# The sixth group's output tails: turned ahead of the quadrant copies, spread by VectorE

## The chip, the cores and the metric

One core of one Trainium2 chip runs the whole kernel. The metric is the device time of one execution in microseconds; the time of a kernel is the median of its runs.

## The reference

```python
B, F, D, L = 16384, 26, 16, 6          # Din = min(F * D, 1024) = 416
def reference(x0, ws, bs):             # x0 (16384, 416), ws (6, 416, 416), bs (6, 416), all bfloat16
    x = x0
    for l in range(L):
        proj = jnp.einsum('bd,de->be', x, ws[l]) + bs[l]
        x = x0 * proj + x
    return x
```

Six layers of a cross network: each multiplies the current rows by a square matrix, adds a bias, multiplies elementwise by the input rows and adds the current rows.

## The kernel before

**Groups, jobs, tiles, tails.** The 16384 rows are eight groups of 2048. Group g in layer l is job (g, l); both count from 0, so the sixth group is g = 5, and its last layer is job (5, 5). On chip the activations are kept transposed: features on partitions, rows along the free dimension. 416 features are three blocks of 128 (tiles 0, 1 and 2 of a job) and a remainder of 32 features, the tail. 2048 rows are four chunks of 512, which is one PSUM bank. The tail of a group is one tensor of 128 partitions x 512: each of the four chunks has its 32 features in one quadrant of 32 partitions. In some groups the chunks change quadrants from layer to layer, and the old tail, which is the residual of the next layer, has to be copied to the new quadrants: `prefill` calls `rotate` (lines 445 and 446), two DMAs for a job on SyncE's queue. These are the quadrant copies.

**One chunk of a tile.** TensorE does 13 matmuls of 32 rows each (lines 1073 and 1077) into a PSUM bank; ScalarE adds the bias and writes a work buffer `tw` (line 551; there are four such buffers, one for a tile); for each pair of chunks VectorE multiplies by x0 (line 563) and adds the current x (line 568). The tails of two or three jobs are done together in `tails` (lines 680 and 692); ScalarE or VectorE reads the result (lines 612, 608), VectorE multiplies and adds (lines 614, 616).

**The order of work.** The queues are written out by hand: `Program.add` appends an instruction to the list of its engine, in the order in which the Python code runs, and works out the semaphore waits from the names of the buffers that are read and written. An engine works its list strictly in order. SyncE's list issues nearly all DMAs. The matmuls' order comes from a string (`ORDER`). In VectorE's list the addition of one pair is held back behind the next multiplication. The last jobs are (5,5), (7,3), (6,4), (7,4), (6,5), (7,5). One batch of tails holds (5,5), (7,3) and (6,4), and the next and last one (7,4) and (6,5). The batch with (5,5) comes behind the first two tiles of (7,3); then come tile 2 of (7,3), the three tiles of (6,4), and the first two of (7,4).

**The output of a group.** A finished group is turned back to rows by transposing DMAs into the buffer `ost` (line 905 for groups 5 and 6, each tile as it is finished), and its tails into a small buffer `ot3` (`turn_rest`, line 900). `spread` copies `ot3` into the last 32 columns of every row of `ost` (line 923 on GpSimd), and `store` writes `ost` out (line 930): in one DMA for group 5, in two halves for group 6. Group 6 uses the same `ost` afterwards. When both the three tiles and the tails of a last layer are done, `done_with` calls `output`.

**The last group.** Job (7, 5) is computed with rows on partitions, so it isn't turned at its end: TensorE (line 1138), ScalarE (line 1187), VectorE's multiplication and addition (lines 1193, 1199), then stores (`nat_store`, line 1206) in five DMAs on SyncE and one on ScalarE's queue. It needs x of layer 5 with rows on partitions: tiles 0 and 1 come from transposing DMAs after the first tiles of (7, 4) (`rest_turn`, line 942), which also wait for a small memset on GpSimd (line 940).

Before the change, SyncE's list behind the batch with (5,5) is: four quadrant copies (two for (7,4), two for (6,5)), the turn of group 5's tails, group 5's store, three `rest_turn` DMAs, the turn of group 6's tails, five turns of group 6's tiles (line 905), the store of its first half, the sixth turn, the first store of the last group, the store of group 6's second half, and the other stores of the last group.

Of the kernel before, what the change touches and what calls it, by code (L numbers as in the profile page):

```python
# [21 lines left out]
class Program:  # L22
# [12 lines left out]
    def add(self, eng, fn, reads=(), writes=(), lane=None, batch=None, hold=False, release=False, row=None):  # L35
        op = Op(eng, fn, lane, batch, row)
        deps = {}
        if eng == "pool":
            writes = list(writes) + ["pool"]
        for t in reads:  # L40
            w = self.writer.get(t)
            if w is not None:
                deps[id(w)] = (w, True)
        for t in writes:
            w = self.writer.get(t)
            if w is not None:
                deps[id(w)] = (w, True)
            for r in self.readers.get(t, ()):
                if id(r) not in deps:
                    deps[id(r)] = (r, False)  # L50
        for d, raw in deps.values():
            if d.lane is None and d.eng == eng and lane is None and (eng == "pe" or not raw):
                if row is None or d.row is None or row == d.row:
                    continue
            op.deps.append(d)
        for t in reads:
            self.readers.setdefault(t, []).append(op)
        for t in writes:
            self.writer[t] = op
            self.readers[t] = []  # L60
        if eng == "dve":
            if hold:
                self.flush()
                self.held = op
            else:
                self.queue[eng].append(op)
                if release:
                    self.flush()
        else:
            self.queue[eng].append(op)  # L70
        if lane is not None:
            batches = self.lanes.setdefault(lane, [])
            if not batches or batches[-1][0] != batch:
                batches.append((batch, []))
            batches[-1][1].append(op)
        return op
# [230 lines left out]
def bass_standalone__cross_network_dcn__recsys_kernel(  # L307
# [7 lines left out]
    L = ws.shape[0]  # L315
    NT = 3
    NJ = 4
# [4 lines left out]
    LAST = NG - 1  # L322
# [58 lines left out]
    def take(n):  # L381
        got = ring[:n]
        ring[:] = ring[n:] + got
        return got
# [11 lines left out]
    def wm_tok(l, i):  # L396
        return ("wm", l) if i < 2 else ("wm", l, "rest")
# [33 lines left out]
    def x03_toks(s):  # L431
        return [("x03q", s, j) for j in range(NJ)]
# [6 lines left out]
    def quad(g, l, j):  # L439
        q = (j + turn_of(g, l)) % NJ  # L440
        return q, slice(q * T32, (q + 1) * T32)
# [22 lines left out]
    def x3_src(g, l):  # L464
        if l == 0:
            s = slot(g)
            return x0s[s][:, XW:XW + CH], x03_toks(s)
        s = xtail[(g, l)]
        return x3s[s][:, :], [("x3", s)]
# [67 lines left out]
    phases, behind_tail, dve = [], [], [0]  # L537
# [134 lines left out]
    def tails(batch, corners_last=False, banks=None):  # L672
        bs_ = banks or take(len(batch))

        def corners():
            for (g, l), b in zip(batch, bs_):
                s3, tok3 = x3_src(g, l)
                for j in range(NJ):
                    (ri, qi), (ro, qo) = quad(g, l, j), quad(g, l + 1, j)
                    add("pe", lambda h, l=l, b=b, s3=s3, ri=ri, qi=qi, ro=ro, qo=qo: h.matmul(  # L680
                        psum[qo, b * CH:(b + 1) * CH], w3[l][qi, NT * P:D], s3[qi, :],
                        start=not corners_last, stop=corners_last, tile_position=(ri * T32, ro * T32)),
                        reads=tok3 + [("w3", l, ri)], writes=[("ps", b)])

        if not corners_last:
            corners()
        for (g, l), b in zip(batch, bs_):
            src, stok = x_src(g, l)
            for t in range(NT):
                for j in range(NJ):  # L690
                    ro, qo = quad(g, l + 1, j)
                    add("pe", lambda h, t=t, j=j, src=src, l=l, b=b, ro=ro, qo=qo: h.matmul(  # L692
                        psum[qo, b * CH:(b + 1) * CH], wm[l][:, t, NT * P:D], src(t, j, j + 1),
                        start=(corners_last and t == 0), stop=(not corners_last and t == NT - 1),
                        tile_position=(0, ro * T32)),
                        reads=[stok(t, j), wm_tok(l, NT)], writes=[("ps", b)])
            if not corners_last:
                evacuate_tail(g, l, b)
        if corners_last:
            corners()  # L700
            for k in sorted(range(len(batch)), key=lambda k: k != 1):
                evacuate_tail(*batch[k], bs_[k], vector=k == 1)
                while behind_tail:
                    behind_tail.pop(0)()
        pr.flush()
        for g, l in batch:
            if corners_last:
                prefill(g, l + 1)
                filled.add((g, l + 1))
        for g, l in batch:  # L710
            if l == L - 1 and g > LAST - 3:
                turn_rest(g)
                if g == LAST - 1:
                    spread("pool")
            done_with(g, l)
        while later:
            load_group(later.pop(0))
# [158 lines left out]
    def output(g):  # L876

        s, s3 = xset[(g, L)], xtail[(g, L)]
        if g < LAST - 1:
            if g < LAST - 2:  # L880
                turn(g, 0)
                turn_rest(g)
            spread("pool")
            if g < LAST - 2:
                turn(g, 1)
                turn(g, 2)
            store(g, 0, NJ)
        free_x.append(s)
        free_3.append(s3)

    def turn(g, t):
        s = xset[(g, L)]
        add("sp", lambda h: h.dma_start_transpose(
            ost[:, :, t * P:(t + 1) * P], xs[s][:, t * GC:(t + 1) * GC]),
            reads=[("x", s, t, j) for j in range(NJ)], writes=[("ost", t, j) for j in range(NJ)],
            lane="ot" if t else "ot0", batch=g)

    def turn_rest(g):
        s3 = xtail[(g, L)]
        add("sp", lambda h: h.dma_start_transpose(ot3[:, :, :], x3s[s3][:, :]),  # L900
            reads=[("x3", s3)], writes=["ot3"], lane="ot3", batch=g)
# [13 lines left out]
    def spread(eng):  # L915

        dst = ost[:, :, NT * P:D].rearrange("p (j k) f -> p j k f", j=NJ)
        sp_ = ot3[:, :, :].rearrange("p k (j f) -> p j k f", j=NJ)
        kw = dict(reads=["ot3"], writes=[("ost", NT, j) for j in range(NJ)])
        if eng == "act":  # L920
            add("act", lambda h: h.activation(dst, sp_, ACT_F.Copy), **kw)
        else:
            add(eng, lambda h: h.tensor_copy(dst, sp_), **kw)  # L923

    def store(g, j0, j1):

        rows = out[g * GC + j0 * CH:g * GC + j1 * CH, :]
        o = ost[:, j0 * KK:j1 * KK, :].rearrange("p (j k) f -> p j k f", k=KK)
        pat = "(j p k) f -> p j k f" if g == 0 else "(j k p) f -> p j k f"
        add("sp", lambda h: h.dma_start(rows.rearrange(pat, j=j1 - j0, k=KK), o),  # L930
            reads=[("ost", t, j) for t in range(NT + 1) for j in range(j0, j1)],
            writes=[("out", g, j0)], lane="out", batch=(g, j0))
# [3 lines left out]
    def rest_turn(t):  # L936

        s = xset[(LAST, L - 1)]
        if t == 0:
            add("pool", lambda h: h.memset(warm[:, :], 0.0), writes=x0_all(s5) + x03_toks(s5) + ["x5 free"])  # L940
        for j0, j1 in ((0, NJ),) if t == 0 else ((0, 2), (2, NJ)):
            add("sp", lambda h, j0=j0, j1=j1: h.dma_start_transpose(
                x5f[:, j0 * KK:j1 * KK, t * P:(t + 1) * P], xs[s][:, t * GC + j0 * CH:t * GC + j1 * CH]),
                reads=[("x", s, t, j) for j in range(j0, j1)] + ["x5 free"],
                writes=[("x5n", j, t) for j in range(j0, j1)], lane=f"x5_{t}{j0}", batch=0)
# [46 lines left out]
    def finish_tile(g, l, n=1, i=0):  # L992
        tiles_done[(g, l)] = tiles_done.get((g, l), 0) + n
        if l == L - 1 and g == LAST - 2:
            turn_out(g, i, 0, NJ)
        elif (g, l) == (LAST, L - 2) and i < NT - 1:
            rest_turn(i)
        if tiles_done[(g, l)] == NT:
            done_with(g, l)

# [126 lines left out]
    g, l = LAST, L - 1  # L1127
# [155 lines left out]
```

## Time and profile before

| what | value |
|---|---|
| time, median of 3 runs | 468.16 us (467.97 to 468.24) |
| profiled execution, its own time | 468.65 us |
| its span, first to last instruction | 466.9 us |
| mean granted TensorE clock | 0.997 |
| HBM | 5.97 MB read, 13.63 MB written |

The profile describes the one execution of 468.65 us; its times count from the start of the span. Each engine has rows of its own, PE for TensorE, PEld for its weight loads, DVE for VectorE, ACT for ScalarE, POOL for GpSimd, and SPq for the instructions by which SyncE issues DMAs. The duration of an SPq row is the time that the issue held SyncE's queue; the transfer itself ends later, and the DMA views give the time from issue to landing and the bytes moved.

### The profile page before, as it was taken

To read this page: it belongs to the slowest core of one execution; us is meant where nothing else is said; L and a number is where in the kernel's file an instruction comes from. 1 tells how busy PE (TensorE), PEld (TensorE's weight loads), DVE (VectorE), ACT (ScalarE), POOL (GpSimd) and SP (SyncE) were. 2 spreads that over 40 slices of the span, in tenths; PEclk is the share of its full clock that TensorE was granted. 3 is DMA by queue.
4 is the path that set the end of the run, shared out by engine and by line. 5 is a ranking of instruction groups with operands and counts; after the bars stand their busy time and mean duration, and the time that the engine had idled before them with its cause. 6 is when DMAs were issued, how large, how long until landed. Compare 5 with 4: busy or idle time off the path is not lost.

```text
span 466.9 us, 17814 instructions
## 1 busy us (share of the span) xinstructions
PE 457.7 (98%) x8001; PEld 266.0 (57%) x8001; DVE 403.5 (86%) x695; ACT 381.8 (82%) x609; POOL 9.5 (2%) x16
## 2 busy tenths in 40 slices
PE   8999999999999999999999999999999999999993
PEld 4344656575656556565665556565556665556551
DVE  1897898988889898898988979898988898989995
ACT  4686889887988888898888888888888897888893
POOL 1000000000000000000000000000000000002000
PEclk9999999999999999999999999999999999999998
DMA  8985859000003949095568619983000094181999
GB/s 225 189 175 138 152 119 196 10 22 12 15 4 36 171 152 190 13 150 160 116 113 126 182 46 170 129 249 104 25 2 4 25 165 132 37 138 37 218 186 275
DMA packets 139152, 53.78 MB, mean 115 GB/s; under 512 B 112826, under 2 KB 138564, under 8 KB 139076
## 3 DMA queue, kind: packets, MB, share of 16 engines
q1 hardware_dynamic: 138920, 52.54, 53.3%
q8 instruction: 62, 1.02, 0.9%
q10 hardware_dynamic: 156, 0.11, 0.1%
q14 instruction: 14, 0.11, 0.1%
HBM read 5.97 MB, written 13.63 MB: 42 GB/s over the span
## 4 chain that ended last, share of the span: by engine, by line
PE 94%; DVE 3%; DMA 1%; issue 0%; SPq 0%; ACT 0%; DVEq 0%
PE ps L1073 73%; PE ps L692 7%; PE ps L1077 6%; PE ps L645 4%; PE ps L639 1%; PE ps L680 1%; DMA wm<-in_ws_dram 1%; DVE x L1199 1%; DVE x L1193 1%; DVE tw L563 1%; PE ps L666 1%; PE ps L789 0%; DVE x L568 0%; SPq L734 0%; ACT tw L551 0%
## 5 line engine op out<-in xcount | busy, mean ns | idle before, releaser
L1073 PE MATMUL ps<-x,wm 32*128 32x512 bf16 x6288 | 372.8, 374 | 0.0
L551 ACT ACTIVATE tw<-ps,bias 128x512 bf16<-128x512 f32 x524 | 326.9, 688 | 48.8 <-PE ps L1073 35.9
L1073 PEld LDWEIGHTS ps<-x,wm 32*128 32x128 bf16 x6288 | 222.2, 92 | 135.2 <-ACT tw L551 6.4
L563 DVE TENSOR_TENSOR tw<-tw,x 128x1024 bf16<-128x1024 bf16 x262 | 177.6, 691 | 40.8 <-ACT tw L551 39.2
L568 DVE TENSOR_TENSOR x<-tw,x 128x1024 bf16<-128x1024 bf16 x262 | 170.8, 687 | 0.3
L1077 PE MATMUL ps<-x,w 32*128 32x512 bf16 x524 | 159.5, 374 | 0.0
L1077 PEld LDWEIGHTS ps<-x,w 32*128 32x128 bf16 x524 | 44.6, 92 | 6.0
L692 PE MATMUL ps<-x,wm 128*32 128x512 bf16 x564 | 33.6, 380 | 0.0
L612 ACT ACTIVATE ts<-ps,bias 128x512 bf16<-128x512 f32 x32 | 20.4, 685 | 13.1 <-PE ps L680 13.1
L515 ACT ACTIVATE tw<-ps,bias 128x1024 bf16<-128x1024 f32 (+1 forms) x24 | 20.7, 937 | 8.2 <-PE ps L666 7.0
L692 PEld LDWEIGHTS ps<-x,wm 128*32 128x32 bf16 x564 | 13.5, 96 | 18.2 <-ACT tw L551 3.7
L645 PE MATMUL ps<-x,wm 128*128 128x512 bf16 x92 | 21.3, 380 | 1.4 <-DMA wm<-in_ws_dram 1.4
L616 DVE TENSOR_TENSOR x<-ts,x 128x512 bf16<-128x512 bf16 x47 | 18.4, 419 | 0.3
L923 POOL COPY ost<-ot 128x512 bf16<-128x512 bf16 x7 | 8.0, 1148 | 433.4 <-DMA ot<-x 433.4
L645 PEld LDWEIGHTS ps<-x,wm 128*128 128x128 bf16 x92 | 8.4, 98 | 12.6 <-issue 2.1
L524 DVE TENSOR_TENSOR tw<-tw,x 128x1024 bf16<-128x1024 bf16 (+1 forms) x21 | 13.0, 636 | 2.2 <-ACT tw L515 2.1
L608 DVE SCALAR_TENSOR_TENSOR ts<-ps,bias,x 128x512 bf16<-128x512 f32 x15 | 11.2, 747 | 3.1 <-PE ps L680 3.1
L529 DVE TENSOR_TENSOR x<-tw,x 128x1024 bf16<-128x1024 bf16 (+1 forms) x21 | 12.6, 634 | 0.0
L614 DVE TENSOR_TENSOR ts<-ts,x 128x512 bf16<-128x512 bf16 x32 | 12.4, 418 | 0.0
L799 DVE COPY x<-ps 128x512 bf16<-128x512 bf16 x5 | 2.0, 422 | 8.8 <-PE ps L789 8.8
L1138 PE MATMUL ps<-wm,x 128*128 128x416 bf16 x48 | 9.3, 340 | 0.0
L1187 ACT ACTIVATE x<-ps 128x416 bf16<-128x416 f32 x16 | 7.7, 528 | 1.5 <-PE ps L1138 1.5
(50 smaller groups left out, 70.8 us busy)
## 6 DMA issues: line engine op xcount, KB each, us to landing
out_dram<-ost SPq DMA_DIRECT2D x6, 1664.0 KB, 8.3
x<-x SPq DMA_DIRECT2D x24, 96.0 KB, 2.2
x<-in_x_dram SPq DMA_DIRECT2D x8, 208.0 KB, 4.8
x<-in_x_dram SPq DMA_DIRECT2D x4, 416.0 KB, 8.3
out_dram<-ost SPq DMA_DIRECT2D x2, 832.0 KB, 4.3
wm<-in_ws_dram SPq DMA_DIRECT2D x5, 312.0 KB, 3.4
x<-x SPq DMA_DIRECT2D x22, 64.0 KB, 2.0
out_dram<-x SPq DMA_DIRECT2D x3, 416.0 KB, 4.9
```

What stands on the lines that cost most here:

```text
L515: add("act", lambda h, a=a, w=w, b0=b0: h.activation(tw[r][:, a * CH:(a + w) * CH], psum[:, b0 * CH:(b0 + w) * CH], ACT_F.Identity, bias=b ...
L524: add("dve", lambda h, a=a, e=e: h.tensor_tensor(tw[r][:, a * CH:e * CH], tw[r][:, a * CH:e * CH], x0s[s0][:, i * GC + a * CH:i * GC + e * ...
L529: add("dve", lambda h, a=a, e=e: h.tensor_tensor(xs[so][:, i * GC + a * CH:i * GC + e * CH], tw[r][:, a * CH:e * CH], src(i, a, e), ALU.ad ...
L551: add("act", lambda h: h.activation(tw[r][:, j * CH:(j + 1) * CH], bank(b), ACT_F.Identity, bias=bias[:, i, l:l + 1], scale=1.0), reads=[( ...
L563: add("dve", lambda h: h.tensor_tensor(tw[r][:, o], tw[r][:, o], x0s[s0][:, c], ALU.mult), reads=[("tw", r, k) for k in both] + [x0_tok(s0 ...
L568: add("dve", lambda h: h.tensor_tensor(xs[so][:, c], tw[r][:, o], src(i, a, a + 2), ALU.add), reads=[("tw", r, k) for k in both] + [stok(i ...
L612: add("act", lambda h: h.activation(ts[r][:, :], bank(b), ACT_F.Identity, bias=bias[:, 3, l:l + 1], scale=1.0), reads=[("ps", b), "bias"], ...
L616: add("dve", lambda h: h.tensor_tensor(x3s[so][:, :], ts[r][:, :], res, ALU.add), reads=[("ts", r)] + rtok, writes=[("x3", so), ("x3", so, ...
L645: add("pe", lambda h, t=t, j=j: h.matmul(bank(banks[j]), wm[l][:, t, ecols], src(t, j, j + 1), start=(first and t == 0), stop=(not first a ...
L692: add("pe", lambda h, t=t, j=j, src=src, l=l, b=b, ro=ro, qo=qo: h.matmul(psum[qo, b * CH:(b + 1) * CH], wm[l][:, t, NT * P:D], src(t, j, ...
L1073: add("pe", lambda h, l=l, t=t, j=j, b=b, q=q, ecols=ecols, src=src, kw=kw: h.matmul(bank(b), wm[l][q, t, ecols], src(t, j, j + 1)[q, :], ...
L1077: add("pe", lambda h, l=l, b=b, q=q, ecols=ecols, s3=s3, kw=kw: h.matmul(bank(b), w3[l][q, ecols], s3[q, :], **kw), reads=tok3 + [("w3", l ...
```

## The change

The call of `turn_rest` (and for group 6 of `spread`) moves in `tails` to a loop of its own ahead of the quadrant copies. For group 5, `output` no longer spreads and stores: behind the end of tile 0 of job (6, 4), `finish_tile` lets VectorE do the spread copy, and then adds group 5's store to SyncE's list. In that list the turn of group 5's tails thus stands ahead of the four quadrant copies, and the store keeps its place, behind them and ahead of the `rest_turn` DMAs. The last batch of tails has no quadrant copies, so for group 6 the lists stay as they are, and its spread stays on GpSimd.

```diff
@@ in tails @@
         pr.flush()
         for g, l in batch:
+            if l == L - 1 and g > LAST - 3:
+                turn_rest(g)
+                if g == LAST - 1:
+                    spread("pool")
+        for g, l in batch:
             if corners_last:
                 prefill(g, l + 1)
                 filled.add((g, l + 1))
         for g, l in batch:
-            if l == L - 1 and g > LAST - 3:
-                turn_rest(g)
-                if g == LAST - 1:
-                    spread("pool")
             done_with(g, l)
@@ in output @@
-        if g < LAST - 1:
-            if g < LAST - 2:
-                turn(g, 0)
-                turn_rest(g)
+        if g < LAST - 2:
+            turn(g, 0)
+            turn_rest(g)
             spread("pool")
-            if g < LAST - 2:
-                turn(g, 1)
-                turn(g, 2)
+            turn(g, 1)
+            turn(g, 2)
             store(g, 0, NJ)
@@ in finish_tile @@
         elif (g, l) == (LAST, L - 2) and i < NT - 1:
             rest_turn(i)
+        elif (g, l, i) == (LAST - 1, L - 2, 0):
+            spread("dve")
+            store(LAST - 2, 0, NJ)
```

## The prediction

> **What bounds the kernel now.** I read the page first, for the engines and the chain of waits, and then the timeline of each engine over the last 50 us, because every instruction that the change touches starts after 421 us.
>
> ```profile
> PE 457.7 (98%) x8001; PEld 266.0 (57%) x8001; DVE 403.5 (86%) x695; ACT 381.8 (82%) x609; POOL 9.5 (2%) x16
> PE 94%; DVE 3%; DMA 1%; issue 0%; SPq 0%; ACT 0%; DVEq 0%
> ```
>
> TensorE carries the chain for 94% of the span. An edit that only shortens work of VectorE or GpSimd in the middle of the stream is worth nothing. What can change is the end, where the chain leaves TensorE, and it does not end at VectorE's last instruction either. The timeline of SyncE's queue (start, duration, line; a duration is the issue, not the transfer; the row of 462.28 is the last of the four in front of it):
>
> ```profile
> 421.19 0.46 SPq L445 DMA_DIRECT2D x<-x  x1
> ...
> 424.73 1.33 SPq L900 DMA_TRANSPOSE ot<-x  x1
> 431.82 0.41 SPq L930 DMA_DIRECT2D out_dram<-ost  x1
> 436.33 3.63 SPq L942 DMA_TRANSPOSE x<-x  x1
> ...
> 440.00 1.30 SPq L942 DMA_TRANSPOSE x<-x  x1
> ...
> 443.38 1.27 SPq L900 DMA_TRANSPOSE ot<-x  x1
> 444.75 7.77 SPq L905 DMA_TRANSPOSE ost<-x  x5
> 452.69 0.47 SPq L930 DMA_DIRECT2D out_dram<-ost  x1
> 453.20 2.13 SPq L905 DMA_TRANSPOSE ost<-x  x1
> ...
> 458.47 0.37 SPq L930 DMA_DIRECT2D out_dram<-ost  x1
> 458.88 4.61 SPq L1206 DMA_DIRECT2D out_dram<-x  x4
> 462.28 1.21 SPq L1206 DMA_DIRECT2D out_dram<-x  x1
> ```
>
> From 436.33 on this queue is packed: each instruction starts within 0.2 us of the end of the one in front, up to 455 us. The queue's own waits say which of its instructions are held by data:
>
> ```profile
> SPq L942 <- DVE ts L608: 7.4, 1, 7.4
> SPq L930 <- DMA ost<-x: 1.5, 1, 1.5
> ```
>
> The first L942 is held by VectorE, not by the queue, so 436.33 does not move. The store at 458.47 is held by the landing of the transpose issued at 453.20, and the four last stores stand behind it. VectorE's rows beside them:
>
> ```profile
> 437.74 1.29 DVE L568 TENSOR_TENSOR x<-tw,x 128x1024 bf16<-128x1024 bf16 x2
> ...
> 451.26 0.69 DVE L568 TENSOR_TENSOR x<-tw,x 128x1024 bf16<-128x1024 bf16 x1
> ...
> 460.83 0.65 DVE L1199 TENSOR_TENSOR x<-x,x 128x416 bf16<-128x416 bf16 x2
> ```
>
> The transpose at 453.20 reads what VectorE had finished at 451.95: 1.25 us late. The last store that SyncE issues reads the first of the two additions at 460.83, done by about 461.2; it is issued at 462.28, 1.0 us late. So SyncE's queue, and what its DMAs carry, set the end. The bytes moved, in 40 slices of 458 to 467 us (0.225 us each):
>
> ```profile
> GB/s 362 340 359 211 4 0 259 355 355 355 340 292 362 355 359 351 355 289 325 366 362 348 333 329 355 373 348 340 333 337 337 344 337 259 15 0 0 0 0 0
> ```
>
> It is empty near 459.1, then full at some 345 GB/s from 459.4 to about 465.7, and then nothing until the span ends at 466.9. The end is a drain, and the drain starts when the store of 458.47 is issued.
>
> Why is the queue late? The same view for 430 to 440 us (0.25 us each) shows the sixth group's store, issued at 431.82:
>
> ```profile
> GB/s 0 0 0 0 0 0 0 0 0 0 0 220 363 353 353 349 356 346 346 349 349 356 346 353 326 329 336 313 398 270 223 214 183 182 106 40 23 18 18 148
> ```
>
> Its data run from 432.75 to about 437.5, over the start of the first L942. That transpose holds the queue for 3.63 us. The same size of transpose with nothing in front of it holds it for:
>
> ```profile
> 408.50 1.95 SPq L905 DMA_TRANSPOSE ost<-x  x1
> ```
>
> **The change part by part.** *The turn is moved ahead of four rotations.* The two halves of VectorE's order around it:
>
> ```profile
> 422.36 0.75 DVE L616 TENSOR_TENSOR x<-ts,x 128x512 bf16<-128x512 bf16 x2
> ...
> 426.96 1.29 DVE L568 TENSOR_TENSOR x<-tw,x 128x1024 bf16<-128x1024 bf16 x2
> ...
> 439.94 0.42 DVE L616 TENSOR_TENSOR x<-ts,x 128x512 bf16<-128x512 bf16 x1
> ```
>
> The first L616 of the pair writes the sixth group's last tails, done by about 422.75. Now the turn is issued there instead of at 424.73. Its landing is one of these (min, median, max of seven):
>
> ```profile
> DMA to landing us min/median/max: 2.5/2.6/4.1
> ```
>
> The old one took the 4.1: GpSimd started at 428.86, and four rotations were in front of it. With none in front I take 2.6, so it lands at 425.4, with 4.1 at 426.9. The four rotations start 1.3 us behind 422.75 instead of at 421.2; they fill the residuals of the next batch of tails, read from 439.94 on, so their delay of some 3 us costs nothing.
>
> *The spread moves from GpSimd to VectorE.* It stands behind the two additions of the first tile of job (6,4). Counting VectorE's instructions in program order from that L616 pair (two multiplications and two additions for each of two tiles), these are the additions at 426.96, which end at 428.25. The landing is 1.3 to 2.8 us earlier than that, so VectorE does not wait. The trace has no such copy on VectorE; the nearest rows are a copy of a quarter of the partitions from SBUF, a full one from PSUM, and the same copy on GpSimd:
>
> ```profile
> L756 DVE COPY x<-ost x4: 284/287/291, 19.4 to 20.3; 32x512 bf16<-32x512 bf16 x4
> L799 DVE COPY x<-ps 128x512 bf16<-128x512 bf16 x5 | 2.0, 422 | 8.8 <-PE ps L789 8.8
> 428.86 2.87 POOL L923 COPY ost<-ot 128x512 bf16<-128x512 bf16 x1 [50.47 <-DMA ot<-x]
> 430.57 0.69 DVE L563 TENSOR_TENSOR tw<-tw,x 128x1024 bf16<-128x1024 bf16 x1
> ...
> 431.32 0.95 DVE L563 TENSOR_TENSOR tw<-tw,x 128x1024 bf16<-128x1024 bf16 x1
> ```
>
> The bounds are 0.29 and 2.87 us; I take 0.42, the same shape on the same engine. What goes away: the multiplication at 431.32, beside GpSimd's copy, took 0.95 where the one in front took 0.69, which gives back 0.26 us. VectorE is up to 0.42 us late from 428.25 to 432, and 0.16 behind that. That is hidden by its waits for ScalarE:
>
> ```profile
> DVE tw L563 <- ACT tw L551: 1.4, 5, 0.3
> ```
>
> These are the waits between 424 and 446 us; 1.4 us of lateness would vanish there. Without that cover it would come one for one onto the stretch after 446, where VectorE has no gaps. What stands behind the copy are the multiplications of (6,4)'s second tile; their readers on ScalarE (a work buffer four tiles on) and TensorE (the job two on) come several us later. SyncE's store now waits for VectorE, and behind it stand only the L942s, which need later VectorE work anyway. GpSimd's memset at line 940, which also frees the L942s, loses the copy in front of it.
>
> *The store.* It is issued at about 428.25 + 0.42 + 0.1 = 428.8 instead of 431.82, 3.0 us earlier. Its data end near 434.5 instead of 437.5: 1.8 us before the first L942 starts.
>
> *The queue behind it.* The first L942 starts at 436.33 as before, and takes 1.95 instead of 3.63. That gives 1.7 us; but the second L942 needs the first addition of the pair at 437.74, done at 438.4, so it starts at 438.45 instead of 440.00: 1.55 us gained. The turn at 443.38 and the five L905 from 444.75 move by about 1.5, with one or two of them near their data. The store of 452.69 moves to 451.2. The transpose of 453.20 cannot start before 451.95: 1.2 us. It stands behind the 832 KB of the store in front, which now run 1.5 us earlier, so its landing moves by 1.2 to 1.5, and with it the store of 458.47. The drain moves by as much: I take 1.4 us.
>
> *Is there room at the end?* VectorE's last additions end at 461.5, and that does not move. The last stores then have to land, 104 KB each. A 64 KB copy (from the page), the store of 458.47 and SyncE's last one (from the DMA view of 458 to 467 us):
>
> ```profile
> x<-x SPq DMA_DIRECT2D x22, 64.0 KB, 2.0
> ...
> out_dram<-ost SPq DMA_DIRECT2D x1, 832.0 KB, 4.0
> ...
> out_dram<-x SPq DMA_DIRECT2D x1, 104.0 KB, 4.0
> ```
>
> In the drain the 4.0 contain a queue of other stores. With 2 us without a queue, they could land at 463.6, under the drain's new end of 465.7 - 1.4 = 464.3. With 4.0 even without a queue they land at 465.3 to 465.5.
>
> The Trainium skill, in DMA: Bandwidth & Descriptors, section "Anatomy of one DMA — SWDGE (gpsimd) path", gives a DMA a fixed part of about 2.0 us, mostly the write receipt, and the rest by bytes; that is written for another issuing path than SyncE's. By it a 104 KB store would take an estimated 2.2 us alone, so the sum would stay a drain, 1.4 us; by the 4.0 of the row as a floor the gain would be 0.9. The 64 KB row agrees with the rule; no run here shows a small store alone.
>
> *The sum.* The span goes from 466.9 to 465.5 us. The profiled execution took 468.65, so 1.75 lie around the span; it would become 467.25. The median of the three runs is 0.5 lower, 468.16, and becomes **466.76**, say 466.8 us. A measurement of this kernel can tell about 0.2%, 0.94 us, from no change: faster means under 467.22, slower over 469.10.
>
> **The rivals.** *A floor under the last landing.* If the last store needs its 4.0 us whatever is in front of it, the end moves only by what SyncE's last issue gains: it starts at 461.25 instead of 462.28, 1.0 us, with ScalarE's own store right behind; 0.9 us, 467.3. For it: the 104 KB store needs as long as the 832 KB one. Against: the GB/s row shows the drain full until 465.7, so it had others in front.
>
> *The queue gives it back.* If the 3.63 us belong to the transpose and not to the store in front, or if later transposes stall for their predecessors until the same moments, nothing moves: 468.1. For it: long issues also appear without a store, as the 2.13 at 453.20. Against: 1.95 for the same size with a free queue.
>
> *Slower: VectorE waits in its order for the turn.* The spread stands in a queue that works without gaps, so a late landing stops all its successors. Landing at T, VectorE is late by T - 428.25 + 0.16, less the 1.4 us of waits; the end then moves by that remainder less the 1.4 gained. It is slower than 469.10 from T = 428.25 - 0.16 + 1.4 + 1.4 + 0.94 = 431.8, 9.1 us after the issue, and one for one beyond: 469.1 and up. A copy as slow as the 2.87 on GpSimd would add 2.45 to that lateness. For it: the old turn needed 4.1 us. Against: even that lands at 426.9.
>
> **How the numbers follow.** The forecast has 0.55, the floor 0.13, no movement 0.20, and the slower case 0.12, more than its rows give, because it also stands for a stall that no row shows. The forecast's own range is 466.2 (the full 1.7 us of the L942 and the 0.3 us by which the copy might be faster or disturb less) to 467.2. The range reaches up through the floor and no movement, to 468.4, and leaves out the slower case and a little at the low end. Faster by over 0.2% takes the forecast without a sliver, and a third of the floor: 0.56. Within 0.2%: the rest of the floor, no movement and the sliver, 0.32. Slower: 0.12.
>
> **What would show it.** In the changed kernel's profile the turn is issued near 422.8 and the sixth store near 428.8, VectorE's copy takes about 0.42 with no wait for a DMA, GpSimd's copies are one fewer, the multiplications near 431 take 0.69, the first L942 holds the queue for about 2.0, the transpose of 453.20 starts near 452.0, the store of 458.47 near 457.1, and the drain ends near 464.3. The prediction is wrong if that L942 still takes over 3 us, if VectorE waits for the turn, or if the bytes stop flowing well before the last landing.

## The result, and the profile after

| | before | changed |
|---|---|---|
| median, 14 runs each | 468.27 us (467.82 to 468.76) | 467.09 us (466.52 to 467.77) |
| span of the profiled execution | 466.9 us | 465.8 us |

The ratio is 0.9975, with a 95% interval of 0.9967 to 0.9983: 1.18 us faster, where 1.4 were forecast. The page's first part and its chain of waits:

```profile
PE 459.0 (99%) x8001; PEld 265.9 (57%) x8001; DVE 402.9 (87%) x696; ACT 382.3 (82%) x609; POOL 6.9 (1%) x15
...
PE 96%; DVE 2%; ACT 1%; issue 0%; DVEq 0%
```

TensorE has the same work as before. One instruction more on VectorE and one fewer on GpSimd are all that the totals show. The difference is in SyncE's queue (start, duration of the issue, line; lines 899, 904, 929, 941 and 1208 of the changed kernel are 900, 905, 930, 942 and 1206 of the one before):

```profile
422.73 1.19 SPq L899 DMA_TRANSPOSE ot<-x  x1
...
428.41 0.41 SPq L929 DMA_DIRECT2D out_dram<-ost  x1
436.27 1.71 SPq L941 DMA_TRANSPOSE x<-x  x1
438.39 1.58 SPq L941 DMA_TRANSPOSE x<-x  x1
440.01 1.49 SPq L941 DMA_TRANSPOSE x<-x  x1
441.55 2.14 SPq L899 DMA_TRANSPOSE ot<-x  x1
443.78 7.71 SPq L904 DMA_TRANSPOSE ost<-x  x5
451.66 0.46 SPq L929 DMA_DIRECT2D out_dram<-ost  x1
452.16 2.11 SPq L904 DMA_TRANSPOSE ost<-x  x1
...
457.37 0.37 SPq L929 DMA_DIRECT2D out_dram<-ost  x1
457.78 4.64 SPq L1208 DMA_DIRECT2D out_dram<-x  x4
```

Group 5's store is issued 3.4 us earlier. The first `rest_turn` issue starts where it did and holds the queue for 1.71 us, not 3.63. By the five turns of group 6's tiles the queue is 0.97 us ahead, and it stays so: 1.10 at the store of group 6's second half. The bytes moved from 458 to 467 us, in 40 slices of 0.225 us:

```profile
GB/s 0 226 359 344 359 344 300 333 381 359 344 355 292 322 377 348 355 344 333 336 355 351 344 348 336 348 329 322 296 30 0 0 0 0 0 0 0 0 0 0
...
out_dram<-x SPq DMA_DIRECT2D x1, 104.0 KB, 4.1
```

The drain ends near 464.5 instead of 465.65, 1.1 us earlier, and the span ends some 1.25 us behind the last byte in both kernels. The last store that SyncE issues (104 KB) still lands 4.1 us behind its issue. VectorE's side, the copy and what follows it:

```profile
428.10 0.28 DVE L922 COPY ost<-ot 128x512 bf16<-128x512 bf16 x1
428.30 1.28 DVE L563 TENSOR_TENSOR tw<-tw,x 128x1024 bf16<-128x1024 bf16 x2
...
430.71 1.28 DVE L563 TENSOR_TENSOR tw<-tw,x 128x1024 bf16<-128x1024 bf16 x2
...
433.74 1.29 DVE L563 TENSOR_TENSOR tw<-tw,x 128x1024 bf16<-128x1024 bf16 x2 [0.55 <-ACT tw L551]
```

The copy starts without a wait and takes 0.28 us, and the pair near 430.7 takes 1.28. At 433.74 VectorE has already waited 0.55 us for ScalarE (0.33 in the kernel before): the copy has not made it late.

### The profile page after: what moved, and what is told of

It reads as the page before. It is cut to its first block, busy times and chain, and to the rows that moved or that the text cites. A ratio compares the mean times of both kernels' runs of the same rounds, so it can differ in the third digit from the quotient of the medians.

```text
span 465.8 us, 17814 instructions
## 1 busy us (share of the span) xinstructions
PE 459.0 (99%) x8001; PEld 265.9 (57%) x8001; DVE 402.9 (87%) x696; ACT 382.3 (82%) x609; POOL 6.9 (1%) x15
## 4 chain that ended last, share of the span: by engine, by line
PE 96%; DVE 2%; ACT 1%; issue 0%; DVEq 0%
PE ps L1075 73%; PE ps L692 7%; PE ps L1079 6%; PE ps L645 5%; PE ps L639 1%; PE ps L680 1%; DVE x L1201 1%; DVE x L1195 1%; PE ps L772 1%; PE ps L790 1%; ACT tw L551 1%; PE ps L666 1%; DVE tw L563 0%; DVE x L568 0%; DVE x L1163 0%
## 5 line engine op out<-in xcount | busy, mean ns | idle before, releaser
L608 DVE SCALAR_TENSOR_TENSOR ts<-ps,bias,x 128x512 bf16<-128x512 f32 x15 | 11.2, 747 | 3.1 <-PE ps L680 3.1
L922 POOL COPY ost<-ot 128x512 bf16<-128x512 bf16 x6 | 5.5, 912 | 390.8 <-DMA ot<-x 390.8
```

## The experiments

Theory A: the gain is that group 5's store has left the DMAs when the first `rest_turn` wants them. Theory B: the gain is that VectorE is no longer disturbed by GpSimd's copy. Behind those stands a question on the end: does the drain of the bytes set it (theory drain), or a time that the last small stores need in any case (theory floor)?

Executions differ by up to 1.1 us in when the first `rest_turn` starts (435.46 to 436.57 us), whatever the edit. So the table gives, beside the medians, the time from that start to the end of the span, in the one profiled execution of each kernel. The series were run at different times and on different chips of this kind; each is compared with runs of the kernel before beside it. "Store" is the issue of group 5's store, "held" the duration of the first `rest_turn` issue. Line numbers differ by a few from kernel to kernel.

| kernel | median us (runs) | kernel before, same runs | ratio, 95% interval | store | held | start of `rest_turn` to end |
|---|---|---|---|---|---|---|
| before | 468.27 (14) | | | 431.82 | 3.63 | 30.6 |
| the change | 467.09 (14) | 468.27 | 0.9975, 0.9967 to 0.9983 | 428.41 | 1.71 | 29.5 |
| e1 turn only | 467.03 (8) | 468.31 | 0.9975, 0.9965 to 0.9986 | 426.61 | 1.71 | 29.4 |
| e2 VectorE only | 467.37 (11) | 468.31 | 0.9982, 0.9973 to 0.9991 | 428.83 | 1.73 | 29.6 |
| e3 store later | 469.61 (5) | 468.31 | 1.0032, 1.0020 to 1.0045 | 433.20 | 4.75 | 32.1 |
| e4 no store | 467.44 (11) | 468.31 | 0.9983, 0.9974 to 0.9992 | none | 1.79 | 29.7 |
| e5 store in between | 467.71 (11) | 468.61 | 0.9982, 0.9973 to 0.9991 | 431.12 | 2.81 | 30.0 |
| e6 order of stores | 466.72 (5) | 468.61 | 0.9961, 0.9949 to 0.9974 | 428.20 | 1.84 | 29.3 |
| e7 whole turn | 466.62 (5) | 468.61 | 0.9957, 0.9944 to 0.9971 | 428.38 | 1.72 | 28.6 |
| e8 e6 and e7 | 466.73 (5) | 468.43 | 0.9966, 0.9952 to 0.9979 | 428.06 | 1.70 | 29.0 |
| e9 the change again | 467.09 (5) | 468.43 | 0.9969, 0.9956 to 0.9981 | 427.82 | 1.83 | 29.2 |
| e10 e7 again | 466.94 (11) | 468.35 | 0.9966, 0.9955 to 0.9977 | 427.61 | 1.73 | 28.8 |
| e11 the change again | 467.27 (12) | 468.35 | 0.9976, 0.9966 to 0.9986 | 428.30 | 1.78 | 29.7 |

**e1: the first part alone.** To the kernel before:

```diff
+        for g, l in batch:
+            if l == L - 1 and g > LAST - 3:
+                turn_rest(g)              # ahead of the quadrant copies
         for g, l in batch:
             if corners_last:
                 prefill(g, l + 1)
 ...
-            if l == L - 1 and g > LAST - 3:
-                turn_rest(g)
-                if g == LAST - 1:
-                    spread("pool")
+            if (g, l) == (LAST - 1, L - 1):
+                spread("pool")
             done_with(g, l)               # group 5: spread("pool") and store, in output
```

> The kernel before with the first part of the change alone: the turn of group 5's tails ahead of the quadrant copies, the spread still on GpSimd and the store right behind it. Theory A (the gain is group 5's store leaving the DMAs before the first rest_turn DMA wants them): the turn lands near 425.4, GpSimd's copy beside a busy VectorE takes up to 2.9 us, the store is issued near 428.3, the first rest_turn issue takes 1.7 to 2.0 us instead of 3.6, and the time is 0.9 to 1.4 us under the kernel before. Theory B (the gain is that GpSimd's copy no longer disturbs VectorE): the copy is still there, so no gain, within 0.3 us.

```profile
425.34 1.70 DVE L563 TENSOR_TENSOR tw<-tw,x 128x1024 bf16<-128x1024 bf16 x2
```

```profile
424.91 0.98 POOL L924 COPY ost<-ot 128x512 bf16<-128x512 bf16 x1 [46.94 <-DMA ot<-x]
```

```profile
426.61 0.68 SPq L931 DMA_DIRECT2D out_dram<-ost  x1
...
435.92 1.71 SPq L943 DMA_TRANSPOSE x<-x  x1
```

1.28 us under the kernel before: the first part alone gives all of the gain. One expectation missed: GpSimd's copy took 0.98 us, not up to 2.9, so the store went out 1.8 us earlier than in the change, to no further effect. The disturbance is there all the same, only earlier: the pair of multiplications at 425.34 takes 1.70 us, as much as the pair at 430.57 did in the kernel before. The full gain with the copy still on GpSimd is against theory B.

**e2: the second part alone.** To the changed kernel: the loop with `turn_rest` goes back behind the quadrant copies.

> The change with its first part undone: the turn stays behind the four quadrant copies, the spread is VectorE's behind the first tile of (6,4), then the store. The turn lands near 428.8, so VectorE waits some 0.7 us for it at 428.1, and the store is issued near 429.2. Theory A: its data leave the DMAs by 435, still ahead of the first rest_turn DMA; 0.9 to 1.3 us under the kernel before, so the first part of the change is not needed for the time. Theory B: as much as the change, 1.2, less what of the 0.7 us isn't covered, so 0.8 to 1.2. If VectorE's wait comes through to the end, the gain is under 0.5.

```profile
428.51 0.29 DVE L921 COPY ost<-ot 128x512 bf16<-128x512 bf16 x1 [0.59 <-DMA ot<-x]
```

VectorE waits 0.59 us in its order for the turn, as expected, and 0.94 us are still gained; the interval overlaps those of e1 and of the change. Either part is enough. Each brings the store forward by some 3 us or more. As both theories expected a gain here, this run does not choose between them.

**e3: the same copy, the store too late.** To the changed kernel:

```diff
-        elif (g, l, i) == (LAST - 1, L - 2, 0):
+        elif (g, l, i) == (LAST - 1, L - 2, 2):
```

> The change with one size altered: VectorE's spread copy and the store stand behind tile 2 of job (6,4) instead of tile 0. The store is issued near 433.5, 1.7 us later than in the kernel before. Theory A: its data run from 434.4 to 439.2, the first rest_turn issue takes about 5.2 us instead of 3.6, and the time is 0.8 to 1.7 us ABOVE the kernel before. Theory B: the copy is on VectorE as in the change, so the gain stays, 1.0 to 1.2 us under.

```profile
433.20 0.41 SPq L929 DMA_DIRECT2D out_dram<-ost  x1
436.08 4.75 SPq L941 DMA_TRANSPOSE x<-x  x1
```

1.30 us slower than the kernel before, inside the range of theory A and on the other side from theory B. The turn is ahead, the copy is VectorE's, and the change is a loss, because the store comes 1.4 us later than before.

**e4: the kernel before without group 5's store.** The store of group 5 is left out of `output` (its rows are not written), and nothing else.

> The kernel before, leaving out group 5's store alone (those output rows are not written); the turn, the quadrant copies and GpSimd's copy are as before. Theory A: the first rest_turn issue takes 1.7 to 2.0 us and the time is 0.9 to 1.4 us under the kernel before, as much as the change gains. Theory B: GpSimd's copy still disturbs VectorE, so within 0.3 us of the kernel before.

```profile
428.34 2.94 POOL L924 COPY ost<-ot 128x512 bf16<-128x512 bf16 x1 [50.40 <-DMA ot<-x]
```

```profile
430.87 0.95 DVE L563 TENSOR_TENSOR tw<-tw,x 128x1024 bf16<-128x1024 bf16 x1
```

```profile
435.88 1.79 SPq L943 DMA_TRANSPOSE x<-x  x1
```

GpSimd's copy is as long as before and VectorE's multiplication as disturbed (0.95 us), and still 0.87 us are gained, a little under the 0.9 to 1.4 of theory A, with the issue held for 1.79. Again the disturbance is there, and the gain too. Leaving the store out altogether gives no more than bringing it forward.

**e5: a size in between.** As e3, with tile 1.

> The change with one size altered: spread and store behind tile 1 of (6,4) instead of tile 0. The store is issued near 430.9, 0.9 us before that of the kernel before, and its data run from 431.9 to about 436.8. Theory A (the first rest_turn issue is held until the store's data are out): that issue takes 2.4 to 3.0 us, between the 1.7 of the change and the 3.6 of the kernel before, and the time is 0.4 to 0.9 us under the kernel before. A theory in which only the engine of the copy counts expects the change's whole 1.2 us.

```profile
431.12 0.41 SPq L929 DMA_DIRECT2D out_dram<-ost  x1
436.57 2.81 SPq L941 DMA_TRANSPOSE x<-x  x1
```

0.90 us under the kernel before, at the upper end of what was expected; the hold of 2.81 is as expected. With e3 and the two kernels this is a row: stores at 428.41, 431.12, 431.82 and 433.20 hold the first `rest_turn` for 1.71, 2.81, 3.63 and 4.75 us, and 29.5, 30.0, 30.6 and 32.1 us are left to the end.

**e6: the drain, by the order of the last stores.** To the changed kernel:

```diff
-    store(LAST - 1, 2, NJ)
     for kk in range(1, KK):
 ...
         if kk < last:
             nat_store(kk, 0, NJ)
+        if kk == 1:
+            store(LAST - 1, 2, NJ)
```

> The change, and in SyncE's list the last group's second store ahead of the store of group 6's second half, which waits for a transpose's landing near 457.4 while the other's data are ready at 456.8. Theory drain (the end is the draining of the stores' bytes): the empty stretch of the DMAs near 458 fills, the bytes end about 1 us earlier, and the time is 0.6 to 1.0 us under that of the change, 1.8 to 2.2 under the kernel before. Theory floor (the last 104 KB stores, issued at 461.2 and 461.5, need their 3.5 to 4.1 us whatever is in front of them): nothing more than 0.2 us under the change.

From the DMA view of 458 to 467 us, and the bytes of the change in the view of 450 to 460 us (0.25 us a slice):

```profile
GB/s 314 274 373 348 337 348 333 329 348 322 318 355 329 355 318 333 344 318 336 336 322 333 337 333 329 322 200 15 0 0 0 0 0 0 0 0 0 0 0 0
...
out_dram<-x SPq DMA_DIRECT2D x1, 104.0 KB, 3.9
```

```profile
GB/s 277 270 228 213 178 171 216 217 202 209 172 347 376 363 346 306 290 373 359 333 243 155 237 247 215 254 301 376 353 346 310 33 0 270 359 349 353 323 316 369
```

The empty stretch is gone, and the bytes end near 464.1. The span ends 1.3 us behind them, as elsewhere. But from the start of `rest_turn` to the end it took 29.3 us, within the 29.2 to 29.7 of the three executions of the change. In the profile, then, the expected 0.6 to 1.0 us below the change is missing. Only about 0.5 us were empty in the change (from 457.8 to 458.3), so there was less to gain than expected; why even that did not come out is not shown. The medians say otherwise: 466.72 is 1.89 us under the kernel before, inside the 1.8 to 2.2 that theory drain expected. But the change was not run beside it, and series differ by nearly as much as it would add (0.7): the kernel of e7 is 1.99 us under the kernel before here and 1.41 in e10. What this edit alone is worth is open.

**e7: one issue fewer in the queue.** To the changed kernel, in `rest_turn`:

```diff
-        for j0, j1 in ((0, NJ),) if t == 0 else ((0, 2), (2, NJ)):
+        for j0, j1 in ((0, NJ),):
```

> The change, and the second rest_turn step (tile 1 of (7,4)) as one DMA instead of two halves: one issue near 2.0 us from 439.0 on instead of 1.6 + 1.5 from 438.4 on. Theory A, in its part that SyncE's queue between 436 and 452 us sets when the drain starts: the queue behind it moves up by about 0.5 us, if no later issue is held longer, and the time is 0.2 to 0.5 us under that of the change. If the queue has slack there, or the held issues only move (as the turn of group 6's tails, 2.1 us instead of 1.3 in the change), no change within 0.2 us.

```profile
438.95 2.05 SPq L941 DMA_TRANSPOSE x<-x  x1
```

```profile
443.06 7.50 SPq L904 DMA_TRANSPOSE ost<-x  x5
450.73 0.46 SPq L929 DMA_DIRECT2D out_dram<-ost  x1
451.88 1.97 SPq L904 DMA_TRANSPOSE ost<-x  x1
...
456.35 0.37 SPq L929 DMA_DIRECT2D out_dram<-ost  x1
```

```profile
GB/s 348 333 314 370 359 351 351 352 351 340 263 392 359 355 340 314 348 351 322 351 340 333 322 333 152 7 0 0 0 0 0 0 0 0 0 0 0 0 0 0
...
out_dram<-x SPq DMA_DIRECT2D x1, 104.0 KB, 2.9
```

28.6 us from the start of `rest_turn`, 0.9 less than the change, where at most 0.5 was expected (e10 has the medians side by side); the queue is 0.7 us ahead at the tile turns and 1.0 at the store of the second half. This is against theory floor as the prediction had it: the last SyncE store of 104 KB is issued at 461.13, as in the change (461.18), but lands 2.9 us behind its issue, where it took 4.1 in the change and 4.0 in the kernel before. With the same kernel it took 3.4 in e10. The backlog in front is shorter: the bytes end near 463.5. So the end moved by a microsecond while the last issue started at the same time.

**e8 and e9: both edits, and the change beside them.**

> The change with both later edits: the second rest_turn step as one DMA, and the last group's second store ahead of the store of group 6's second half. Theory drain: the empty 0.7 us near 457 that is left with the first edit fills, the bytes end near 463.1, and the time is 0.3 to 0.7 us under that edit alone, 2.3 to 2.8 us under the kernel before. Theory floor, in its weaker form (a 104 KB store needs the 2.9 us that it took with the first edit): the last store, issued at 461.4, lands at 464.3 as it did, and the time stays within 0.2 us of that edit alone, 1.8 to 2.2 under the kernel before.

> The change itself once more, on the same chip as the kernel with both later edits, so that the two can be compared: 1.0 to 1.4 us under the kernel before, whichever theory.

```profile
454.17 2.63 SPq L1208 DMA_DIRECT2D out_dram<-x  x2
456.96 0.39 SPq L929 DMA_DIRECT2D out_dram<-ost  x1
```

The bytes in e8 from 450 to 460 us:

```profile
GB/s 211 205 218 209 170 253 366 373 359 366 353 346 310 296 363 240 219 228 219 183 258 357 353 363 356 177 0 0 0 186 356 310 246 379 353 346 363 349 346 353
```

Both edits together are 1.70 us under the kernel before, less than the 2.3 to 2.8 of theory drain; the 29.0 us from the start of `rest_turn` lie between e7 and the change. The two edits do not add up, and the rows say why: the last group's second store now stands in front of group 6's second half, which is issued at 456.96, not at 456.35 as in e7. That second store waits for VectorE's addition of 455.81 (0.59 long) and is issued at 456.42, so the empty stretch, which was to fill, is 1.0 us long, where it is about 0.5 in e7. On top of e7 the order of the two stores is an exchange, not a gain. Theory floor in its weaker form, a store that needs e7's 2.9 us, expected e8 within 0.2 us of e7, and 466.73 against 466.62 (in another series) agrees; but as the stretch did not fill, e8 cannot rule it in or out. Against the change in the same series, 466.73 to 467.09, the intervals overlap. The change itself is 1.34 us under the kernel before here and 1.08 in e11, as expected.

**e10 and e11: e7 and the change side by side.**

> The change with the second rest_turn step as one DMA, now on the same chip as the change itself. From the start of the first rest_turn issue to the end of the span it took 28.6 us against 29.2 to 29.5 for the change and 30.5 for the kernel before; if that difference is the edit's, the time is 0.5 to 0.9 us under that of the change. If it was the spread between chips, within 0.2 us.

> The change itself, beside the kernel above: 1.0 to 1.4 us under the kernel before; 29.2 to 29.6 us from the start of the first rest_turn issue to the end of the span.

The median of e7's kernel is 0.33 us under the change's, 466.94 to 467.27, between the 0.5 to 0.9 of an effect and the 0.2 of none, and the intervals overlap. In the profiles it is 28.8 against 29.7 us. It is faster than the kernel before; that it beats the change points the same way in both comparisons, but is not settled.

## Why the prediction was right

**The bound.** That the end is a drain held by SyncE's queue was right: in all thirteen profiled executions the span ends 1.2 to 1.3 us behind the last byte, however the edit moved the two. The time alone did not show it: 1.18 us lie midway between the 1.4 of the forecast and the 0.9 of the floor, and in the change the last store was issued at 461.18 and took 4.1 us, just as the floor had it. E7 decides, where the same store, issued at the same time, took 2.9.

That VectorE sets the start of the first `rest_turn` was right, but not by the row that was read for it. That row names L608, which starts at 438.95, inside the issue of 436.33, and cannot have let it start. The addition that can is this one, before and in the change:

```profile
435.02 1.29 DVE L568 TENSOR_TENSOR x<-tw,x 128x1024 bf16<-128x1024 bf16 x2
```

```profile
434.95 1.28 DVE L568 TENSOR_TENSOR x<-tw,x 128x1024 bf16<-128x1024 bf16 x2
```

It ends at 436.31 and 436.23, and the issue starts at 436.33 and 436.27.

**The turn and the spread.** The turn was issued at 422.73 (422.75 was said) and landed 2.5 us later (2.6 was taken); the view of all seven such turns has

```profile
DMA to landing us min/median/max: 2.5/2.6/3.4
```

VectorE did not wait. The copy cost 0.285 us at 428.1, where 0.42 was taken: the row of the small copy, 0.287, was the right neighbour, not the copy from PSUM. The Trainium skill, in the page VectorE: DVE Perf Modes, section "The TRN2 errata — SBUF-src ops pay a fixed extra latency per instruction", has a measured fixed term of about 150 cycles and takes a bf16 copy in SBUF at 4x; an estimate by it is (150 + 512/4) / 0.96 GHz = 290 ns, and the trace agrees. The relief of VectorE was larger than said as well: the pair that took 1.70 us takes 1.28. Neither reached the end, as forecast. The store went out at 428.41 (428.8).

**The first `rest_turn`.** 1.71 us against 1.95 forecast, and the cause that the prediction gave, the sixth group's store in front, is shown by runs: the hold follows the store's place in four sizes (e3, e5, the change, the kernel before), and falls to 1.79 when the store is left out (e4).

**What was mis-sized: the queue behind it.** The prediction let 1.5 us pass unchanged to the tile turns. In the profiles 1.92 us go in at the first issue, and 0.91 come out, counted from the start of the first `rest_turn` to the first tile turn (8.42 us before, 7.51 after). The second issue waits 0.41 us for VectorE, which was foreseen. At the turn of group 6's tails the queue is still 1.83 us ahead (441.55 against 443.38). But this turn, 1.27 us long before, is held for 2.14. In the kernel before, the long one is the third `rest_turn` issue:

```profile
441.35 1.99 SPq L942 DMA_TRANSPOSE x<-x  x1
```

In the change that one takes 1.49. A hold has moved from one issue to the next. The prediction named this as a rival ("or if later transposes stall for their predecessors"), and took it as all or nothing; it took 0.6 of the forecast 1.5 us. With 0.97 us at the tile turns and 1.10 at the store of the second half, instead of 1.5 and 1.4, the end moved by 1.1 to 1.2. E7, with one transpose fewer there, reaches the first tile turn in 6.83 us.

**The rivals.** A floor of 4.0 us under the last landing is out: it took 2.9 us in e7 and 3.4 in e10. A lower one is not. The queue giving all back is out. The slower case, VectorE stopped by a late turn, came about in e2 in a small size: it waited 0.59 us, and the gain stayed. A wait beyond the 1.4 us that the prediction took as cover was not tried. The sign did turn once, in e3, not by any of the rivals but by the prediction's own mechanism the other way round: the store issued later, and the hold longer.

**Still open.** What sets the hold of the third or fourth transpose in a row (1.99 before, 2.14 in the change, 2.57 in e5) was not tried on its own. Whether the last stores have a floor near 2.9 us is open: the one on ScalarE's queue took 2.9 to 3.0 in e7, e8 and e10. Why GpSimd's copy takes 0.98 us at 424.91 and 2.94 at 428.34, both beside a busy VectorE, is open too.

## What to carry to other kernels

A store that nobody waits for can still cost time at its other end: here, while its data filled the DMAs, the next transposing DMA of the same queue held that queue for up to 4.75 us instead of 1.7, and everything in order behind it (no run tried another queue). So look in the issuing queue for issues that are longer than their like, see in the bytes moved what was in flight then, and move that transfer, not the issue. If the kernel ends in a drain of stores, ask what starts the drain: here its start came 1.10 us earlier and the time fell by 1.18. Reordering the stores in it is less sure: on top of e7 it put one in the place of another (e8), and alone it showed nothing in the profile (e6).

## What the runs showed of the hardware that was not expected

The issue of one and the same transpose held SyncE's queue for 1.71 to 4.75 us, by what stood in front of it in the DMAs (1.79 with no store at all). And a spread copy of 128x512 bf16 in runs of 32 elements took 0.285 us on VectorE, as long as the 32x512 copy with no such runs (0.287), and, for group 5, 0.98 to 2.94 us on GpSimd.
